# Row sums and second pooled product of each visit in 64x64 tiles, and sums of v by seven full matmuls

## The chip, the cores and the metric

The kernel runs on one core of one Trainium2 chip. The metric is the device time of one launch in microseconds (us), taken as the median over runs. TensorE is called PE in the views, VectorE DVE, ScalarE ACT, GpSimd POOL, and SyncE SP; PEld is TensorE's loading of weights.

## The reference

q, k and v have the shape (8 batches, 8 heads, 576 positions, 64). Two attentions are computed for each head and added, and a two-layer block with SiLU follows.

```python
def _attn_ref(q, k, v):
    factor, Sd, scale = 4, S // 4, 1.0 / np.sqrt(D)
    q_d = q.reshape(B, H, Sd, factor, D).mean(axis=3)     # k_d, v_d alike
    out_d = sm_attn(q_d, k_d, v_d)                        # softmax attention of the 144 pooled rows
    out_up = np.repeat(out_d, factor, axis=2)
    mask = np.abs(pos[:, None] - pos[None, :]) < factor   # a band of 7 positions
    attn = softmax(np.where(mask, scale * q @ k.T, -1e9))
    return out_up + attn @ v

def _moe_ref(x, w_in, w_out):                             # x: 4608 x 512
    h = x @ w_in                                          # 512 -> 2048
    return (h * sigmoid(h)) @ w_out                       # 2048 -> 512
```

## The kernel before, in words

The 64 heads are handled as 32 pairs (two heads of one batch). For a pair p these steps exist, each with its TensorE matmuls, and after them the steps of other engines:

- `T{p}` (`pe_T`): 36 transposes of q and k (L810), evicted by ACT (L565) and then pooled by DVE (L845) into `qd` and `kd`. POOL issues the loads of later pairs' q and k (L676) into buffers that a T frees.
- `S{p}` (`pe_S`): 28 score matmuls (20 of the band, 8 of the pooled rows); ACT takes the exponentials into `Pt` (band) and `Pd` (pooled) (L893), and DVE multiplies `Pt` by the band's mask (L899, called k below).
- `Z{p}` (`pe_Z`): 12 matmuls with the 0/1 columns of `hot` as weights give the row sums of `Pt` and `Pd`; DVE transposes them out of PSUM (`zt`, L964), takes reciprocals (`zr`, L968) and spreads them (`Rb`, L974).
- `PV{p}` (`pe_PV1` and `pe_PV2`): 20 matmuls of `Pt` with v, then 4 and 4 of `Pd` with the pooled v. DVE scales the product by `Rb` (L990), POOL adds the two attentions into `xT` (L1018).
- `VP{p}` (`pe_VP`, only for the first eight pairs): 9 matmuls with the 0/1 matrix `vsel` as weights sum v over groups of four rows; ACT or DVE evicts them into `vd`. For later pairs POOL makes these sums itself (L785, L790).

A matmul has a tile on the 128x128 array: 64x64 (64 rows of the operands, 64 outputs; four such tiles work side by side), 128x64 (two side by side) or 128x128. S, T, PV1 and the first four `Pd` products are 64x64, Z and the last four `Pd` products (`pe_PV2`) are 128x64, the two layers are 128x128, and VP has five matmuls in 128x128 and four in 128x64.

From pair 8 on, the steps of three pairs are put together in a visit `V{n}` on PE, in the order S of pair n, T of pair n+1, PV1 of pair n-2, Z of pair n-1, PV2 of pair n-2. The row sums go to columns 360 to 455 of the second of the two PSUM banks that also hold the PV product. Between visits PE works on the two layers: G1 (groups of 4 matmuls 128x512 with `w_in_sb`, then tanh on ACT, L1043, and the gate on DVE, L1047) and G2 (groups of 4 with `w_out_bf` and `gT`, evicted by ACT, L1100). There are 576 and 592 such matmuls; the last 32 of G2 are of 256 columns.

All orders come from a planner (`Plan.run`) that runs through a list of jobs with costs and due times written into the kernel, and that emits each engine's instructions in the order so found. Nothing of it is decided on the chip. The planner also puts some matmuls of zeros and ones (`dz`) into idle places of the beginning. A job's cost and its marks (when, within a visit, its parts count as finished) only steer this order. Every matmul goes through `mm` (L571).

Of the kernel before, what the change touches and what calls it, by code (L numbers as in the profile page):

```python
# [9 lines left out]
F32 = mybir.dt.float32  # L10
BF16 = mybir.dt.bfloat16
# [15 lines left out]
VP_PE = 8  # L27

SPLIT = 8
CAST2 = 4  # L30
SW = tuple(range(1, NPAIR))
MB = 8
# [16 lines left out]
def D(p, left):  # L49
    return (22 + 1.5 * (p - 3) if p < 4 else 42 + 3 * (p - 7) if p < 8 else 45 + 8 * (p - 7)) - left  # L50
# [444 lines left out]
def bass_hourglass_attn__then__act_silu_kernel(  # L495
# [9 lines left out]
    with kctx:  # L505
        E = kctx.enter_context
        L = Plan()
        P = Prog()
# [31 lines left out]
        kd = sb("kd", [128, 192], BF16, N_T)  # L540
        Pt = sb("Pt", [128, 2, 288], BF16, N_P)
        Pd = sb("Pd", [128, 2, 216], BF16, N_P)
        zt = sb("zt", [128, 96], F32, N_ZR)
        zr = sb("zr", [128, 24], F32, N_ZR)
        Rb = sb("Rb", [128, 768], F32, N_RB)
        xo = sb("xo", [128, 2, 360], F32, N_XO)
# [12 lines left out]
        hot = sb("hot", [128, 3, 68], BF16)  # L559
# [7 lines left out]
        def half(j):  # L567
            return slice(64 * j, 64 * j + 64)

        def mm(out_, lhsT, rhs, r, w, start, stop):  # L570
            P.op("PE", lambda t: t.matmul(out_, lhsT, rhs, start=start, stop=stop, skip_group_check=True), r, w)  # L571

        S = L.slot

# [38 lines left out]
        def constants():  # L613
# [41 lines left out]
            for i, c in enumerate((CO, CO, CO2)):  # L655
                ts(f"vsel{i}", vsel[:, i, :], cpv[:, i % 2, :], 1.5, ALU.is_le, col(c), ALU.mult, rc(c) + rp,
                   [R(f"vsel{i}")], 0.33, ["cpa", "co", "co2"], 7.6)
            fill("pads", [(t[:, a:b], 0.0, [], [R(f"{n}{i}")]) for i in range(N_T)
                          for t, n, a, b in ((kT[i], "kTa", 0, 3), (kT[i], "kTb", 579, 592), (kd[i], "kdp", 144, 192))], -75)
            fill("hot", [(hot[:, i, :], 0.0, [], [R(f"hot{i}")]) for i in range(3)]  # L660
# [135 lines left out]
        def bank(key):  # L796
            return L.bind["bank", key]
# [123 lines left out]

        def after_VP(p):
            def emit(jb):
# [37 lines left out]
        def after_Z(p, key, i, col_):  # L961
            def emitt(jb):
                z, b = S("zr", p), bank(key)[i]
                P.op("DVE", lambda e: e.transpose(zt[z][:, :], PS[:, b, col_:col_ + 96]), [rB[b]], [R(f"zt{z}")])  # L964

            def emit(jb):
                z = S("zr", p)
                P.op("DVE", lambda e: e.reciprocal(  # L968
                    zr[z][:, :].rearrange("p (c b) -> p c b", b=3),
                    zt[z][:, :].rearrange("p (b c) -> p c b", b=3)[:, 0:8, :]), [R(f"zt{z}")], [R(f"zr{z}")])  # L970
# [6 lines left out]
            J(f"zt{p}", "DVE", 0.23, emitt, pre=[f"Z{p}"], bank=[(key, ())], take=[("zr", p)], due=D(p, 4.0))  # L977
# [151 lines left out]
        def split(p):  # L1129
            J(f"T{p}", "PE", 0.42, lambda jb: pe_T(p), mm=36, kind="A", due=D(p, 8.5), **tk(p))  # L1130
            after_T(p)
            if p >= SPLIT:
                return
            J(f"S{p}", "PE", 0.46, lambda jb: pe_S(p), mm=28 + 4 * (p < MB), kind="A", due=D(p, 6.5), **sk(p))
            after_S(p)
            kz = ("z", p)
            J(f"Z{p}", "PE", 0.40, lambda jb: pe_Z(p, bank(kz)[0], 0, True), mm=14, kind="A", due=D(p, 4.5), bank=[(kz, Z_BANKS(p))], **zk(p))
            after_Z(p, kz, 0, 0)
            if p < VP_PE:
                J(f"VP{p}", "PE", 0.68, lambda jb: pe_VP(p), mm=9, kind="A", due=D(p, 4.0), use=[("vb", p)], pre=[f"cv{p}", "vsel0", "vsel1", "vsel2"],  # L1140
                  bank=[(("v", p), V_BANKS(p))])
                after_VP(p)

            def emit(jb):
                bb = bank(("o", p))
                pe_PV1(p, bb)
                pe_PV2(p, bb)
            J(f"PV{p}", "PE", 0.57, emit, mm=28, kind="A", due=D(p, 2.4), bank=[(("o", p), O_BANKS(p))], **merge(vk(p), dict(pre=[f"r{p}"])))
            after_PV(p)

        def visit(n):
            s, t = n < NPAIR, n + 1 < NPAIR
            z = n - 1 if SPLIT <= n - 1 < NPAIR else None
            pv = n - LAG if SPLIT <= n - LAG < NPAIR else None
            marks, at_, kw = {}, 0.0, []
            nm = 28 * s + 36 * t + 28 * (pv is not None) + 14 * (z is not None)
            if s:
                at_ += 0.38
                marks[f"S{n}"] = at_
                kw.append(sk(n))  # L1160
            if t:
                at_ += 0.3
                marks[f"T{n + 1}"] = at_
                kw.append(tk(n + 1))
            if pv is not None:
                at_ += 0.25
                kw.append(vk(pv))
            if z is not None:
                at_ += 0.38
                marks[f"Z{z}"] = at_  # L1170
                kw.append(zk(z))
            if pv is not None:
                at_ += 0.13
                marks[f"PV{pv}"] = at_
            zkey = ("o", pv) if pv is not None else ("zz", n)
            kw.append(dict(bank=[(zkey, (CD,))]))

            def emit(jb):
                if s:
                    pe_S(n)  # L1180
                if t:
                    pe_T(n + 1)
                if pv is not None:
                    pe_PV1(pv, bank(("o", pv)))
                if z is not None:
                    pe_Z(z, bank(zkey)[1], 360, pv is None)
                if pv is not None:
                    pe_PV2(pv, bank(("o", pv)))
            J(f"V{n}", "PE", at_, emit, mm=nm, kind="V", due=n, marks={a: min(1.0, b / at_) for a, b in marks.items()}, thr=8 * (n - THR0),
              **merge(dict(pre=[f"V{n - 1}"] if n > SPLIT else []), *kw))  # L1190
            if s:
                after_S(n)
            if t:
                after_T(n + 1)
            if pv is not None:
                after_PV(pv)
            if z is not None:
                after_Z(z, zkey, 1, 360)


        constants()
# [95 lines left out]
```

## Time and profile before

| what | value |
|---|---|
| median of 3 runs | 341.94 us (341.03 to 342.71) |
| the profiled execution, its own time | 342.31 us |
| its span in the profile | 340.5 us, granted clock 0.97 in the mean |
| matmuls on PE | 4623, each with a weight load |
| stretch up to 11.4 us | loads, constants, first transposes |
| 11.4 to 36.3 us | pairs 0 to 3, no G1 yet |
| 36.3 to 74.9 us | pairs 4 to 7 between groups of G1 |
| 74.9 to 279 us | the visits V8 to V33 between groups of G1 and G2 |
| 279 us to the end | G1 and G2 alone |

Times in the views are in us from the start of the span. A line of the timeline gives the start, the time from first start to last end, the engine, the line of code, the operation, what it writes and reads, its tile, its shape and how many instructions were merged. The ends of matmuls overlap with the next starts, so the cost of a group is read from start to start. In square brackets stands the idle time before and what ended it.

### The profile page before, as it was taken

Reading aid. Unit: us, or ns where it says so; the run is one execution under the profiler, and the core shown is the slowest. Engines: PE = TensorE matmul, PEld = TensorE weight load, DVE = VectorE, ACT = ScalarE, POOL = GpSimd, SP = SyncE. Lnnn points to the kernel's source line nnn. Section 1 sums busy time; section 2 is a strip of 40 time slices with the busy share of each in tenths; the row PEclk is TensorE's granted clock in tenths of the full one; section 3 lists DMA queues with packets and bytes.
Section 4 is the critical chain, followed back from the end, with each engine's and each line's share of the span. In section 5 each row is a group of like instructions: output and inputs, shape, how many; then the busy total and the mean of one; then the engine's idle time right before and its main releaser. Section 6 shows DMA issues by size and latency. Waiting matters only on the chain.

```text
span 340.5 us, 10780 instructions
## 1 busy us (share of the span) xinstructions
PE 326.8 (96%) x4623; PEld 213.9 (63%) x4623; DVE 229.6 (67%) x410; ACT 179.0 (53%) x317; POOL 156.6 (46%) x211
## 2 busy tenths in 40 slices
PE   5587999999999999999999999999999999999996
PEld 2465677865555775587557755785577558866544
DVE  6586989866667885788577857796767556754200
ACT  5542756665544765476447645664656416644221
POOL 7363498435679667970698068704400140000000
PEclk9755999999999999999999999999999999999999
DMA  8997879999878976996398339500100010000112
GB/s 168 175 252 156 255 181 212 198 229 234 172 178 195 213 177 151 209 202 174 76 240 180 81 57 249 115 1 33 66 31 2 33 64 31 2 1 31 62 64 92
DMA packets 70666, 44.59 MB, mean 131 GB/s; under 512 B 45914, under 2 KB 63770, under 8 KB 70618
## 3 DMA queue, kind: packets, MB, share of 16 engines
q1 hardware_dynamic: 56378, 28.00, 30.8%
q0 software_dynamic: 13088, 15.36, 26.2%
q8 instruction: 36, 0.59, 0.7%
q10 hardware_dynamic: 1152, 0.54, 0.7%
q14 instruction: 12, 0.10, 0.1%
HBM read 45.61 MB, written 9.44 MB: 162 GB/s over the span
## 4 chain that ended last, share of the span: by engine, by line
PE 92%; DMA 2%; DVE 2%; issue 2%; POOL 1%; ACT 0%; POOLq 0%
PE PS L571 89%; PE PS L810 3%; DMA qkb<-in_k_dram 2%; DVE Pt L899 1%; POOL qkb L676 0%; DVE qd L845 0%; POOL gT L601 0%; DVE Rb L974 0%; DVE qT L565 0%; DVE kd L845 0%; DVE zt L964 0%; DVE zr L968 0%; ACT osb L1076 0%; DVE vd L565 0%; POOL idw L610 0%
## 5 line engine op out<-in xcount | busy, mean ns | idle before, releaser
L571 PE MATMUL PS<-xT,w_in_sb 128*128 128x512 f32 x576 | 141.2, 399 | 0.0
L571 PE MATMUL PS<-w_out_bf,gT 128*128 128x512 bf16 (+1 forms) x592 | 131.3, 374 | 0.0
L571 PEld LDWEIGHTS PS<-xT,w_in_sb 128*128 128x128 f32 x576 | 106.7, 188 | 24.7 <-DVE gT L1047 0.7
L1047 DVE SCALAR_TENSOR_TENSOR gT<-th,PS 128x512 bf16<-128x512 f32 x144 | 96.9, 683 | 37.0 <-ACT th L1043 36.3
L1043 ACT ACTIVATE th<-PS 128x512 f32<-128x512 f32 x144 | 86.1, 599 | 54.2 <-PE PS L571 46.0
L571 PEld LDWEIGHTS PS<-w_out_bf,gT 128*128 128x128 bf16 x592 | 54.7, 98 | 62.9 <-issue 3.5
L1018 POOL TENSOR_TENSOR xT<-xo 128x576 fp32r<-128x576 f32 (+5 forms) x48 | 43.5, 919 | 51.5 <-DVE xo L990 51.4
L565 POOL CAST vb<-vs 128x640 bf16<-128x640 f32 x32 | 24.4, 767 | 57.3 <-PE PS L571 42.5
L1100 ACT ACTIVATE osb<-PS 128x512 f32<-128x512 f32 x35 | 21.1, 603 | 53.6 <-PE PS L571 53.6
L893 ACT ACTIVATE Pt<-PS 128x576 bf16<-128x576 f32 x32 | 20.8, 649 | 33.0 <-PE PS L571 32.8
L785 POOL TENSOR_TENSOR vt<-vq 128x512 f32<-128x512 f32 x24 | 30.8, 1285 | 10.0 <-DMA vq<-in_v_dram 9.9
L990 DVE TENSOR_TENSOR xo<-PS,Rb 128x720 f32<-128x720 f32 x32 | 28.6, 893 | 5.1 <-PE PS L571 4.9
L974 DVE STREAM_TRANSPOSE Rb<-zr 128x768 f32<-128x768 f32 x32 | 30.9, 964 | 0.1
L899 DVE TENSOR_TENSOR Pt<-Pt,mask 128x576 bf16<-128x576 bf16 x24 | 16.3, 677 | 20.9 <-ACT Pt L893 20.9
L565 ACT ACTIVATE qT<-PS 128x576 bf16<-128x576 bf16 x30 | 19.8, 659 | 9.4 <-PE PS L810 9.4
L810 PE MATMUL PS<-idn,qkb 64*64 64x64 bf16 x1152 | 17.5, 201 | 7.5 <-issue 3.9
L845 DVE TENSOR_REDUCE qd<-qT 128x144 bf16<-128x576 bf16 x32 | 22.9, 716 | 1.5 <-ACT qT L565 1.4
L845 DVE TENSOR_REDUCE kd<-kT 128x144 bf16<-128x576 bf16 x32 | 23.0, 718 | 0.0
L964 DVE STREAM_TRANSPOSE zt<-PS 128x96 f32<-128x96 f32 x32 | 8.8, 274 | 20.2 <-PE PS L571 20.2
L565 ACT ACTIVATE kT<-PS 128x576 bf16<-128x576 bf16 x30 | 20.0, 665 | 1.6 <-PE PS L810 1.6
L810 PEld LDWEIGHTS PS<-idn,qkb 64*64 64x64 bf16 x1152 | 14.2, 115 | 9.5 <-issue 4.5
L676 POOL DMA_DIRECT2D qkb<-in_k_dram x31 | 17.1, 553 | 5.1 <-PE PS L810 5.1
(56 smaller groups left out, 229.3 us busy)
## 6 DMA issues: line engine op xcount, KB each, us to landing
vs<-in_v_dram SPq DMA_DIRECT2D x123, 80.0 KB, 4.6
out_dram<-osb SPq DMA_DIRECT2D x35, 256.0 KB, 3.6
vq<-in_v_dram SPq DMA_DIRECT2D x24, 256.0 KB, 4.3
qkb<-in_q_dram POOLq DMA_DIRECT2D x31, 144.0 KB, 5.0
qkb<-in_k_dram POOLq DMA_DIRECT2D x30, 144.0 KB, 5.4
w_in_sb<-in_moe_w_in_dram POOLq DMA_DIRECT2D x4, 1024.0 KB, 7.4
w_out_bf<-in_moe_w_out_dram POOLq DMA_DIRECT2D x4, 512.0 KB, 14.3
vq<-in_v_dram SPq DMA_DIRECT2D x48, 32.0 KB, 3.9
```

The costliest lines, as they stand in the source:

```text
L565: return e.activation(out_, in_, AF.Copy) if eng == "ACT" else e.tensor_copy(out_, in_)
L571: P.op("PE", lambda t: t.matmul(out_, lhsT, rhs, start=start, stop=stop, skip_group_check=True), r, w)
L785: P.op("POOL", lambda g: g.tensor_tensor(vt[:, :, :], vq[n][:, :, 0:128], vq[n][:, :, 128:256], ALU.add), [R(f"vqm{n}"), R(f"vqe{n}0"), R( ...
L810: P.op("PE", lambda e, o=o, w=w, j=j: e.transpose(o, w, idn[half(j), :]), [R("idn"), R(f"qkb{n}{x}")], [rB[t]])
L845: P.op("DVE", lambda e: e.tensor_reduce(dst, src.rearrange("p (g r) -> p g r", r=4), AX.X, ALU.add), [R(f"{'qk'[x]}T{s}")], [R(f"{'qk'[x]} ...
L893: P.op("ACT", lambda e: e.activation(d[:, :, :], PS[:, b[0]:b[1] + 1, a:e_], AF.Exp, scale=sc), [rB[b[0]], rB[b[1]]], [R(f"P{m}" if local ...
L974: P.op("DVE", lambda e: e.transpose(Rb[n][:, :].rearrange("p (c q) -> p c q", q=32), zr[z][:, :].unsqueeze(2).to_broadcast([128, 24, 32])) ...
L990: P.op("DVE", lambda e: e.tensor_tensor(xo[x][:, :, :], PS[:, bb[0]:bb[1] + 1, 0:360], Rb[u][:, :].rearrange("p (x c) -> p x c", x=2)[:, : ...
L1018: P.op("POOL", lambda g, dst=dst, in0=in0, in1=in1: g.tensor_tensor(dst, in0, in1, ALU.add), [R(f"xo{x}")], xblk(kc, t + a, t + e_))
L1043: P.op("ACT", lambda e: e.activation(th[x][:, :], PS[:, b, :], AF.Tanh, scale=0.5), [rB[b]], [R(f"th{x}")])
L1047: P.op("DVE", lambda e: e.scalar_tensor_tensor(gT[j % 2][:, f, :], th[x][:, :], 1.0, PS[:, b, :], ALU.add, ALU.mult), [rB[b], R(f"th{x}")] ...
L1100: P.op("ACT", lambda e, s=S("osb", n), b=bank(key)[0]: e.activation(osb[s][:, :], PS[:, b, :], AF.Copy, scale=0.5), [rB[bank(key)[0]]], [R ...
```

## The change

In the visits V9 to V31 the row sums and the second pooled product are done in 64x64 tiles. A matmul over 128 rows becomes two over 64 rows. Half j of the rows writes to bank j ("straight"); where the result for the other bank is needed as well, four matmuls with the banks exchanged ("cross") are put behind T, and the first of them waits on a semaphore until the last straight one has ended (`fence`). Of Z, the band's sums and the sums over the last 16 pooled rows now lie in both banks, four row columns in each, so DVE transposes 2 x 96 columns (`zt` is 192 wide); the reciprocal writes the same 24 numbers as before. The order of a visit becomes S, PV1, PV2 straight, Z straight, T, PV2 cross, Z cross; in V31, which has no T, S takes T's place. A visit has 120 matmuls in place of 104 where all parts are there (V10 to V30), V9 has 88 in place of 76, and V31 84 in place of 68. V32 and the first eight pairs keep `pe_Z` and `pe_PV2` as they were.

`pe_VP` replaces its four 128x64 matmuls by two of 128x128, with weights `vend` that ACT copies from `vsel` once, behind its first eviction of q and behind the second pair's evictions. The planner's costs of visits are lowered with it. In the order that comes out, PE has V11 and V18 one group of G2 or G1 later; DVE, in many visits from V11 on, takes L990 ahead of `zt`, and k and the pooling of q ahead of the reciprocal or the `Rb` step, where the order was the other way, and some of these change places with gates of G1 next to them; ACT has some evictions of `kT` behind one of `osb`; POOL and SP have some loads and casts one place earlier or later.

```diff
-        zt = sb("zt", [128, 96], F32, N_ZR)
+        zt = sb("zt", [128, 192], F32, N_ZR)
+        vend = sb("vend", [128, 2, 128], BF16)
...
         def mm(out_, lhsT, rhs, r, w, start, stop):
-            P.op("PE", lambda t: t.matmul(...), r, w)
+            P.op("PE", lambda t: t.matmul(...), r, w, after=fence[:])
+            fence[0] = None
...
             for i in (3, 4):                                    # pe_VP
-                x, sh = (1, 43) if i == 3 else (2, 58)
-                for y in range(2):
-                    one(PS[half(y), b, 128:256], vsel[:, x, 186 - sh:250 - sh], x, i, i == 3, i == 4)
+                mm(PS[:, b, 128:256], vend[:, i - 3, :], vb[n][:, i:i + 6:5, :], [R("vend"), R(f"vb{n}")], [rB[b]], i == 3, i == 4)
...
+        def pe_PV2h(p, bb, cross):
+            m, d = S("P", p), S("vd", p)
+            for h in range(2):
+                for j in range(2):
+                    x = 1 - j if cross else j
+                    mm(PS[half(h), bb[x], 288:360], vd[d][half(j), 2 * h, :], Pd[m][half(j), h, 72 * x:72 * x + 72],
+                       [R(f"vd{d}"), R(f"Pd{m}")], [rB[bb[x]]], False, cross)
+
+        def pe_Zh(p, bb, col_, fresh, cross):
+            m = S("P", p)
+            if cross:
+                seq = [(1, 4, Pd[m], (72, 0), "hot1", f"Pd{m}")]
+            else:
+                seq = [(0, 3 - s, Pt[m], (96 * s, 96 * s), "hot0", f"P{m}") for s in range(3)]
+                seq += [(1, 4, Pd[m], (0, 72), "hot1", f"Pd{m}"), (2, 0, Pd[m], (144, 144), "hot2", f"Pd{m}")]
+            for n, (i, w, src, a, rw_, rp_) in enumerate(seq):
+                c = 72 if cross or i == 2 else 96
+                for h in range(2):
+                    for j in range(2):
+                        x, u = (1 - j if cross else j), w + (4 * j if i != 1 else 0)
+                        mm(PS[half(h), bb[x], col_:col_ + c], hot[half(j), i, u:u + 64], src[half(j), h, a[j]:a[j] + c],
+                           [R(rw_), R(rp_)], [rB[bb[x]]], fresh and n == 0, cross)
...
+                bb = bank(zkey)                                 # visit, new = s and z is not None
+                if pv is not None:
+                    pe_PV1(pv, bb)
+                    pe_PV2h(pv, bb, False)
+                pe_Zh(z, bb, 360, pv is None, False)
+                own = P.streams["PE"][-1]
+                if t:
+                    pe_T(n + 1)
+                else:
+                    pe_S(n)
+                fence[0] = own
+                if pv is not None:
+                    pe_PV2h(pv, bb, True)
+                pe_Zh(z, bb, 360, False, True)
```

More of the change, by code (lines that the diff above doesn't have):

```diff
@@ L29 @@
 SPLIT = 8
+VE, VDUE = 'ACT', 12
 CAST2 = 4
@@ L558, in bass_hourglass_attn__then__act_silu_kernel @@
         nidn = sb("nidn", [128, 64], BF16)
-        hot = sb("hot", [128, 3, 68], BF16)
+        hot = sb("hot", [128, 3, 72], BF16)
         idw = sb("idw", [128, 128], BF16)
         vsel = sb("vsel", [128, 3, 207], BF16)
+        vend = sb("vend", [128, 2, 128], BF16)
         cv = sb("cv", [128, 16], F32)
@@ L570, in mm @@
         def mm(out_, lhsT, rhs, r, w, start, stop):
-            P.op("PE", lambda t: t.matmul(out_, lhsT, rhs, start=start, stop=stop, skip_group_check=True), r, w)
+            P.op("PE", lambda t: t.matmul(out_, lhsT, rhs, start=start, stop=stop, skip_group_check=True), r, w,
+                 after=fence[:])
+            fence[0] = None
+        fence = [None]
         S = L.slot
@@ L657, in constants @@
                    [R(f"vsel{i}")], 0.33, ["cpa", "co", "co2"], 7.6)
+            for i, a in enumerate((143, 128)):
+                const(f"vend{i}", VE, {"ACT": 0.3, "POOL": 0.3}[VE], lambda e, i=i, a=a: copy(
+                    VE, e, vend[:, i, :].rearrange("p (y c) -> p y c", y=2), vsel[:, i + 1, a:a + 64].unsqueeze(1).to_broadcast([128, 2, 64])),
+                      r=[R(f"vsel{i + 1}")], w=[R("vend")], pre=[f"vsel{i + 1}"], due=VDUE)
             fill("pads", [(t[:, a:b], 0.0, [], [R(f"{n}{i}")]) for i in range(N_T)
@@ L976, in emitb @@
                     zr[z][:, :].unsqueeze(2).to_broadcast([128, 24, 32])), [R(f"zr{z}")], [R(f"Rb{n}")])
-            J(f"zt{p}", "DVE", 0.23, emitt, pre=[f"Z{p}"], bank=[(key, ())], take=[("zr", p)], due=D(p, 4.0))
+            J(f"zt{p}", "DVE", 0.34 if two else 0.23, emitt, pre=[f"Z{p}"], bank=[(key, ())], take=[("zr", p)], due=D(p, 4.0))
             J(f"r{p}", "DVE", 0.26, emit, pre=[f"zt{p}"], use=[("zr", p)], due=D(p, 3.9))
@@ L1139, in split @@
             if p < VP_PE:
[L1140 removed]
+                J(f"VP{p}", "PE", 0.68, lambda jb: pe_VP(p), mm=7, kind="A", due=D(p, 4.0), use=[("vb", p)], pre=[f"cv{p}", "vsel0", "vsel1", "vsel2", "vend0", "vend1"],
                   bank=[(("v", p), V_BANKS(p))])
@@ L1155, in visit @@
             marks, at_, kw = {}, 0.0, []
-            nm = 28 * s + 36 * t + 28 * (pv is not None) + 14 * (z is not None)
+            new = s and z is not None
+            if new:
+                nm = 28 * s + 36 * t + 32 * (pv is not None) + 24
+            else:
+                nm = 28 * s + 36 * t + 28 * (pv is not None) + 14 * (z is not None)
             if s:
-                at_ += 0.38
+                at_ += 0.37
                 marks[f"S{n}"] = at_
                 kw.append(sk(n))
+            if new:
+                at_ += 0.19 + 0.225 * (pv is not None)
             if t:
@@ L1165, in visit @@
             if pv is not None:
-                at_ += 0.25
+                at_ += 0.03 if new else 0.25
                 kw.append(vk(pv))
             if z is not None:
-                at_ += 0.38
+                at_ += 0.03 if new else 0.38
                 marks[f"Z{z}"] = at_
                 kw.append(zk(z))
+            if new:
+                at_ += 0.1
+                marks[f"Z{z}"] = at_
             if pv is not None:
-                at_ += 0.13
+                at_ += 0.0 if new else 0.13
                 marks[f"PV{pv}"] = at_
@@ L1178, in emit @@
             def emit(jb):
-                if s:
+                if s and (t or not new):
                     pe_S(n)
+                if not new:
+                    if t:
+                        pe_T(n + 1)
+                    if pv is not None:
+                        pe_PV1(pv, bank(("o", pv)))
+                    if z is not None:
+                        pe_Z(z, bank(zkey)[1], 360, pv is None)
+                    if pv is not None:
+                        pe_PV2(pv, bank(("o", pv)))
+                    return
+                bb = bank(zkey)
+                if pv is not None:
+                    pe_PV1(pv, bb)
+                    pe_PV2h(pv, bb, False)
+                pe_Zh(z, bb, 360, pv is None, False)
+                own = P.streams["PE"][-1]
                 if t:
                     pe_T(n + 1)
+                else:
+                    pe_S(n)
+                fence[0] = own
                 if pv is not None:
[L1184 to L1188, printed above, removed]
+                    pe_PV2h(pv, bb, True)
+                pe_Zh(z, bb, 360, False, True)
             J(f"V{n}", "PE", at_, emit, mm=nm, kind="V", due=n, marks={a: min(1.0, b / at_) for a, b in marks.items()}, thr=8 * (n - THR0),
@@ L1197, in visit @@
             if z is not None:
-                after_Z(z, zkey, 1, 360)
+                after_Z(z, zkey, 2 if new else 1, 360)
         constants()
```

20 lines of the change are left out of this document (15 added, 5 removed).

## The prediction

> **What bounds the kernel now.** I read the page first: shares of engines, slices, chain of waits.
>
> ```profile
> PE 326.8 (96%) x4623; PEld 213.9 (63%) x4623; DVE 229.6 (67%) x410; ACT 179.0 (53%) x317; POOL 156.6 (46%) x211
> PEclk9755999999999999999999999999999999999999
> PE 92%; DMA 2%; DVE 2%; issue 2%; POOL 1%; ACT 0%; POOLq 0%
> ```
>
> PE is busy for 96% of the span and carries 92% of the chain, at full granted clock from the fifth slice on. So what PE saves in a visit is saved at the end, unless a new wait takes it. Next comes the timeline of PE over one visit, with the layer matmuls behind it.
>
> ```profile
> 168.38 0.35 PE L571 MATMUL PS<-qT,kT 64*64 64x58 bf16 x20
> 168.56 0.27 PE L571 MATMUL PS<-qd,kd 64*64 64x144 bf16 x8
> 168.66 0.48 PE L810 MATMUL PS<-idn,qkb 64*64 64x64 bf16 x36
> 168.95 0.35 PE L571 MATMUL PS<-Pt,vb 64*64 64x58 bf16 x20
> 169.12 0.22 PE L571 MATMUL PS<-Pd,vd 64*64 64x72 bf16 x4
> 169.27 0.32 PE L571 MATMUL PS<-Pt,hot 128*64 128x96 bf16 x6
> 169.42 0.28 PE L571 MATMUL PS<-Pd,hot 128*64 128x96 bf16 x6
> 169.54 0.23 PE L571 MATMUL PS<-Pd,vd 128*64 128x72 bf16 x4
> 169.71 4.49 PE L571 MATMUL PS<-w_out_bf,gT 128*128 128x512 bf16 x20
> 174.13 0.35 PE L571 MATMUL PS<-qT,kT 64*64 64x58 bf16 x20
> ```
>
> Read from start to start, the visit takes 169.71 - 168.38 = 1.33 us and recurs every 5.75. In 64x64 tiles 36 transposes take 0.29, 8.1 ns each or 0.032 per four. The four `Pd` products at 169.12 should take the same 0.03, but 0.15 pass before the first row sum: 0.12 is the change to 128x64. The second six row sums take 0.12 (0.04 a pair), the first six 0.15. The last four products take 0.17, where pairs at 72/96 of 0.04 need 0.06: 0.11 is the change to 128x128.
>
> **Part 1, Z and PV2 in the visits.** Removed: from the end of the first `Pd` products (169.15) to 169.71, 0.56 us. Added: 32 matmuls of 64x64 in groups of four: four groups of 96 columns, one of 72 (Z straight), one of 72 (PV2 straight), two of 72 behind T. No row shows 96 columns in 64x64. The group of 64 columns takes 0.032; the eight `qd,kd` matmuls take 0.10 for a group of 144 and one of 72, which leaves 0.066 for 144. Between these 96 columns take 0.044; the bounds are 0.032 and 0.066. Sum: 4 x 0.044 + 4 x 0.033 + 0.11 for the one change of tile left = 0.42. Saved 0.14 per visit (0.05 to 0.19), the same in V9 and V31. 23 visits give **-3.2 us** (-1.2 to -4.3).
>
> **Part 2, the fence.** The first cross matmul waits for the last straight one; queued behind it are the other cross matmuls and the next layer group, and `zt` and L990 on DVE wait for these. A 64x64 matmul of 72 columns lasts 203 ns in the groups, and ACT's exponential at 168.88 starts some 0.05 after the S before it ends, so the release comes about 0.25 after the last straight start. T lies between: 36 transposes, 0.29 (in V31 S, 0.28). So it costs **0**, with 0.04 to spare. If the release took 0.1 longer, 23 x 0.06 = 1.4 us; with no cover at all 0.25 x 23 = 5.8.
>
> **Part 3, what moves.** T ends some 0.43 later in the visit (about 169.59 in this one, not 169.14). ACT evicts it from 169.84, as it is busy with the exponentials until then: no loss. POOL's loads of q and k wait for T, and are buffered pairs ahead. PV1 and Z come earlier, but read what DVE and POOL finished in the visit before. `zt` doubles: 0.274 us for 96 columns; bounded by 0 and by twice, I take +0.1, as `Rb` needs 964 ns for 768. DVE's `kd` ended at 173.04 and S used it at 174.31, so 1.27 us cover that. The cover is thinner in G1 right after a run of visits, where DVE works without a break, 0.67 a gate beside a group of 0.91:
>
> ```profile
> 189.57 2.68 DVE L1047 SCALAR_TENSOR_TENSOR gT<-th,PS 128x512 bf16<-128x512 f32 x4
> ```
>
> PE already waits on such gates ten times, 2.7 us of weight loads in the list of waits, mostly hidden. PE comes 0.14 earlier and DVE 0.1 later per visit: 0 to 0.3 for each of four runs; I take **+0.3** in all (0 to 1.2).
>
> **Part 4, VP.** The first four VPs lie where PE waits anyway ("issue" of 1.1 to 2.1 us at 16.6, 21.9, 28.4): 0. The other four:
>
> ```profile
> 39.14 0.69 PE L571 MATMUL PS<-vb,vsel 128*128 128x128 bf16 x9
> 39.76 0.32 PE L571 MATMUL PS<-mbias,nidn 64*64 64x288 bf16 x4
> 47.08 0.69 PE L571 MATMUL PS<-vb,vsel 128*128 128x128 bf16 x9
> 47.70 1.21 PE L571 MATMUL PS<-xT,w_in_sb 128*128 128x512 f32 x4
> ```
>
> Nine take 0.62. Seven of 128 columns, at a quarter of the 0.22 of a 512-column one, take 0.39, and then a change of tile (0.11) at 39.76, or up to that much for the first f32 weights at 47.70: 0.12 saved each. At 38.27 Z follows in the same 128x64, so nothing is saved there. **-0.4 us** (-0.1 to -0.7). The two `vend` copies fall into ACT's idle 1.39 and 1.07 us of the first pairs: 0.
>
> **Part 5, a stall that may go.** In V10 PE waits for `kd`, because k took 2.54 us (0.40 to 0.46 in most visits) while POOL ran casts and sums:
>
> ```profile
> 81.37 2.54 DVE L899 TENSOR_TENSOR Pt<-Pt,mask 128x576 bf16<-128x576 bf16 x1
> 86.48 0.29 PE L571 MATMUL PS<-qd,kd 64*64 64x144 bf16 x8 [0.59 <-DVE kd L845]
> ```
>
> S's first part took 0.94 here, 0.18 elsewhere: 0.76 lost. POOL's cast at 81.63 follows loads that wait for T, which now ends 0.2 later, so k may get through first. Half of it: **-0.4 us**; ends -0.76 and +0.8 (k runs into POOL in another visit).
>
> **Part 6, code.** PE gets 22 x 16 + 12 - 16 = 348 more matmuls and as many weight loads. Its code comes in pieces:
>
> ```profile
> q8 instruction: 36, 0.59, 0.7%
> ```
>
> 9246 PE instructions against 36 transfers are 257 each, so 696 more are nearly three more. At 209.96 a visit stood for half a microsecond on "issue" in mid-visit; in these runs 248 instructions pass per 5.75 us, and 280 will per 5.61. I take **+0.3** (-0.5, that stall gone, to +2.5, one more in each run).
>
> **Sum.** -3.2 + 0 + 0.3 - 0.4 - 0.4 + 0.3 = -3.4. Against the profiled execution's 342.31 (span 340.5 and 1.8 around it) that is 338.9. That execution is 0.37 above the median of 341.94, so I predict 338.5.
>
> **A rule against it.** The Trainium skill, "TensorEngine Tiling (Array Packing)", section "Instruction Overhead", says that every matmul costs about 60 cycles, so that one with a single column takes as long as one with 60. At the 2.4 GHz of its page "TensorE: Matmul & The Clock Gate" that is an estimated 25 ns, and 32 matmuls would take 0.8 us in place of 0.31. This trace does not agree: its 36 transposes take 8.1 ns each.
>
> **Rivals.** (a) *Each matmul has its own price.* If the 32 matmuls took the 20 ns that a row sum takes now (six in 0.12), the part would be 0.64 + 0.11 = 0.75 against 0.56: 23 x 0.19 = 4.4 us more, less 0.8 from parts 4 and 5: 345.5. It decides from 14 ns each ((0.56 - 0.11)/32). For it: no row has 64x64 row sums, and the two halves of the rows read one tile. Against: 8.1 and 9 ns in T and S. The rule above is this case; 5%. (b) *Code becomes the bound in runs of visits.* A piece of 256 now lasts 5.9 us there and will last 5.13. The three stalls of the start ended 5.4 and 6.5 us apart, so a piece can take that long when loads are dense. At 5.4, 24 pieces lose 0.27 each, 6.5 us: 344.7. It decides from 5.3. Against: with 5.9 us between them only one of some 24 pieces was late; 7%. (c) *The gain is eaten, no change.* The fence costs 0.06, DVE 0.3 per run, code one stall per run: 338.5 + 1.4 + 0.9 + 1.2 = 342.0; 17%. (d) *The planner's new order alone*, V11 and V18 a group later, costs or gives nothing by itself, as PE has other work ready; it is within the range.
>
> **How the numbers follow.** My forecast has 71%: -5.1 (all good ends of parts 4 to 6 with 3.2) gives 336.8; the fence, half of DVE's bound and one more code stall give 341.2. With part of (c) the range 336.8 to 341.3 holds 8 in 10. A measurement can tell about 0.5%, 1.7 us, from no change: faster is below 340.2, slower above 343.6. Faster 0.71, same 0.17, slower 0.12 (a and b).
>
> **What would show it.** Right: visits of 1.19 us from S to the next layer group, a period of 5.61, no 128x64 rows from 92 us to 270, groups of four row sums 0.04 apart, a cross matmul within 0.01 of T's end, `zt` at 0.37, VPs of 0.5. Wrong: an idle time before the cross matmuls, "issue" in several visits, new waits of PE on `kd` or on gates, or row sums 15 ns or more apart.

## The result and the profile after

The changed kernel takes 339.04 us in the median of 21 executions (337.98 to 342.57), beside 341.24 us for the kernel before (21 executions): a ratio of 0.9945 (95% interval 0.9925 to 0.9964), so 2.2 us faster. The forecast of 338.5 lies 0.54 below, and its range holds the median. Its saving of 3.4 us was too large all the same: the median of the three runs that the forecast set out from lay 0.7 above this median of 21. A second series of the changed kernel (below) gave 340.12 beside 341.37, 1.25 us.

The profiled execution took 338.79 us, with a span of 337.0. From its page, in the order of the prediction's lines (shares of engines, PE's clock by slices, chain of waits, transfers of PE's code):

```profile
PE 325.8 (97%) x4971; PEld 212.5 (63%) x4971; DVE 234.5 (70%) x410; ACT 179.9 (53%) x319; POOL 154.5 (46%) x211
...
PEclk9755999999999999999999999999999999999999
...
q8 instruction: 39, 0.64, 0.8%
...
PE 95%; DMA 2%; issue 2%; POOL 1%; ACT 0%; POOLq 0%
```

PE still carries the chain, with 348 more matmuls and three more pieces of code. DVE's share rose from 67% to 70%, 4.9 us of work, though only `zt` was meant to grow, by 23 x 0.1 = 2.3 us. The timeline of PE over one visit that nothing held up (V29):

```profile
240.14 0.35 PE L573 MATMUL PS<-qT,kT 64*64 64x58 bf16 x20
240.32 0.27 PE L573 MATMUL PS<-qd,kd 64*64 64x144 bf16 x8
240.42 0.32 PE L573 MATMUL PS<-Pt,vb 64*64 64x58 bf16 x20
240.58 0.24 PE L573 MATMUL PS<-Pd,vd 64*64 64x72 bf16 x8
240.64 0.32 PE L573 MATMUL PS<-Pt,hot 64*64 64x96 bf16 x12
240.78 0.26 PE L573 MATMUL PS<-Pd,hot 64*64 64x96 bf16 x8
240.85 0.48 PE L820 MATMUL PS<-idn,qkb 64*64 64x64 bf16 x36
241.15 0.22 PE L573 MATMUL PS<-Pd,vd 64*64 64x72 bf16 x4
241.18 0.22 PE L573 MATMUL PS<-Pd,hot 64*64 64x72 bf16 x4
241.34 1.04 PE L573 MATMUL PS<-w_out_bf,gT 128*128 128x512 bf16 x4
```

From start to start this visit takes 1.20 us (1.192 unrounded), as forecast. The twelve row sums of `Pt` take 0.13, 0.043 per four; the cross matmul starts 0.30 after T does, which is T's own length. But few visits look so. V19, the first of its run, in the same timeline:

```profile
160.22 0.35 PE L573 MATMUL PS<-qT,kT 64*64 64x58 bf16 x20
...
160.96 0.60 PE L820 MATMUL PS<-idn,qkb 64*64 64x64 bf16 x36
161.37 0.23 PE L573 MATMUL PS<-Pd,vd 64*64 64x72 bf16 x4
...
161.56 3.63 PE L573 MATMUL PS<-w_out_bf,gT 128*128 128x512 bf16 x16
```

T begins 0.74 after S here (0.71 in V29) and lasts 0.41 instead of 0.30: 1.34 us in all. The trace of instructions shows why: T's weight loads have waits of their own, for the loads of q and k and for its freed banks, and waits that do not fit into the weight load are instructions of PE's stream, which show where the stream has no lead: in V19 one of 0.05 us stands between T's first two weight loads, which start 0.125 us apart. Of the visits V10 to V30 only V19, V23, V27 and V30, the first ones of later runs, have such a one in T, and they take 1.33 to 1.40 us.

To see where the time went, PE's starts are summed by kind from V8's first matmul to the last matmul. In the profiles of the experiments the first record of a G2 group is missing behind 21 visits and behind six stretches of G1. In before and after, where none is missing, the second matmul of such a group starts 0.226 us behind the first, and that is taken off the visit or the stretch ahead each time and counted as G2. G2 is then 121.97 to 121.99 everywhere but in e4, where it is 123.66. e1 is not in the table: its profiled execution ran slower, at a granted clock of 0.93, and took 345.65 us.

| profile | V8 starts | V8 to last matmul | visits | mean of V10 to V30 | G1 |
|---|---|---|---|---|---|
| before | 74.88 | 262.68 | 33.46 | 1.402 | 107.24 |
| after | 73.69 | 260.39 | 30.19 | 1.258 | 108.21 |
| e2 visits alone | 75.42 | 260.76 | 30.38 | 1.266 | 108.40 |
| e3 fence uncovered | 74.35 | 267.26 | 37.52 | 1.590 | 107.76 |
| e4 T's waits early | 74.36 | 269.97 | 36.82 | 1.574 | 109.49 |
| e5 the same, code shifted | 73.92 | 259.74 | 29.49 | 1.221 | 108.28 |
| e6 after, code shifted | 74.67 | 260.40 | 30.43 | 1.270 | 107.98 |
| e7 old order | 75.19 | 260.84 | 30.25 | 1.261 | 108.61 |
| e8 after, code shifted more | 74.94 | 262.78 | 32.31 | 1.273 | 108.48 |
| e9 k first | 73.86 | 259.26 | 30.15 | 1.256 | 107.13 |
| e10 k first and e5 | 75.60 | 259.43 | 29.99 | 1.249 | 107.47 |
| e11 after again | 74.01 | 260.62 | 30.58 | 1.277 | 108.07 |
| e12 before, k first | 74.46 | 261.99 | 33.07 | 1.384 | 106.94 |

The profiled pair differs by 3.5 us of span: 1.2 before V8, 3.3 in the visits, and 1.0 given back in G1. Two questions follow: what the visits lose against 1.19 us, and why groups of G1 that nobody changed take longer.

### The profile page after: what moved, and what is told of

The parts are those of the page before. It is cut to its first block, busy times and chain, and to the rows that moved or that the text cites. A ratio compares the mean times of both kernels' runs of the same rounds, so it can differ in the third digit from the quotient of the medians.

```text
span 337.0 us, 11476 instructions
## 1 busy us (share of the span) xinstructions
PE 325.8 (97%) x4971; PEld 212.5 (63%) x4971; DVE 234.5 (70%) x410; ACT 179.9 (53%) x319; POOL 154.5 (46%) x211
## 4 chain that ended last, share of the span: by engine, by line
PE 95%; DMA 2%; issue 2%; POOL 1%; ACT 0%; POOLq 0%
PE PS L573 91%; PE PS L820 4%; DMA qkb<-in_k_dram 2%; POOL gT L607 0%; POOL qkb L686 0%; ACT osb L1119 0%; POOL idw L616 0%; POOL cv L607 0%; POOLq L607 0%; POOLq L1350 0%
## 5 line engine op out<-in xcount | busy, mean ns | idle before, releaser
L1061 POOL TENSOR_TENSOR xT<-xo 128x576 fp32r<-128x576 f32 (+5 forms) x48 | 41.7, 883 | 52.1 <-DVE xo L1033 52.1
L567 POOL CAST vb<-vs 128x640 bf16<-128x640 f32 x32 | 23.0, 723 | 55.1 <-PE PS L573 42.0
L909 DVE TENSOR_TENSOR Pt<-Pt,mask 128x576 bf16<-128x576 bf16 x24 | 19.1, 798 | 22.3 <-ACT Pt L903 22.3
L820 PE MATMUL PS<-idn,qkb 64*64 64x64 bf16 x1152 | 18.3, 202 | 6.0 <-issue 4.0
L800 POOL TENSOR_TENSOR vd<-vt 128x256 bf16<-128x256 f32 x24 | 19.0, 794 | 0.5
```

The lines of the kernel that those rows point to most:

```text
L567: return e.activation(out_, in_, AF.Copy) if eng == "ACT" else e.tensor_copy(out_, in_)
L820: P.op("PE", lambda e, o=o, w=w, j=j: e.transpose(o, w, idn[half(j), :]), [R("idn"), R(f"qkb{n}{x}")], [rB[t]])
L1061: P.op("POOL", lambda g, dst=dst, in0=in0, in1=in1: g.tensor_tensor(dst, in0, in1, ALU.add), [R(f"xo{x}")], xblk(kc, t + a, t + e_))
```

## The experiments

**Each half alone.** e1 keeps the old visits, e2 the old `pe_VP`.

```diff
-            new = s and z is not None
+            new = False                                 # e1_vp_only
```
```diff
-                mm(PS[:, b, 128:256], vend[:, i - 3, :], ...)
+                x, sh = (1, 43) if i == 3 else (2, 58)  # e2_visits_only
+                for y in range(2):
+                    one(PS[half(y), b, 128:256], vsel[:, x, 186 - sh:250 - sh], ...)
```

> Only the sums of v by seven matmuls and the two copies of weights; the visits are as before. In the profiled pair V8 starts at 73.7 us where it was 74.9. Theory (the seven matmuls shorten the stretch where PE has work all the time, 36 to 57 us): two VPs of 0.38 in place of 0.62 and two saved 0.1 or less, V8 0.5 to 0.7 us earlier relative to the first layer group, the time 0.4 to 0.7 us below before (ratio 0.998 to 0.999). Rival (the start decides: when pieces of code and loads arrive): V8's start scatters by 1 us or more from execution to execution, and the time is the same as before or moves by more than 1 us either way.

> Only the visits are changed; VP keeps its nine matmuls. Theory (gains add up): from V8 to the end 2.3 us shorter than before as in the changed kernel's profile (265.6 to 263.3), the time 1.5 to 2.3 us below before, ratio 0.993 to 0.996. Rival (most of the measured gain came from the start): less than 0.8 us, ratio above 0.9975.

e1 took 340.87 us, ratio 0.9976 (0.9951 to 1.0001); e2 took 340.27, ratio 0.9966 (0.994 to 0.9992), beside 341.36 before. The halves, 0.5 and 1.1 us, add up to about what the whole saves; e1's interval holds 1, so its half is not shown by the times alone. e2 fell short of the 1.5 to 2.3 us expected: the visits bring one third of their -3.2 in the median. e2's profile has the same losses as after's: visits of 1.266 in the mean and G1 at 108.40. VP has nothing to do with them.

**The fence without its cover.** T goes back behind S, so that nothing lies between the last straight and the first cross matmul.

```diff
                 pe_S(n)
+                pe_T(n + 1)                             # e3_fence_bare
                 ...
                 pe_Zh(z, bb, 360, pv is None, False)
-                pe_T(n + 1)
                 fence[0] = own
```

> As the changed kernel, but T goes back to its place behind S, so nothing lies between the last straight row sum and the cross matmuls that wait for it. Theory (release 0.25 us after the last straight start, hidden by T's 0.29): an idle time of about 0.25 us before the cross matmuls in 22 visits (V31 keeps its cover), less 0.02 to 0.1 because T's own waits are then passed while PE still works on the layer matmuls; visits of 1.40 us, 4 to 5 us above the changed kernel, 1 to 2 us above before. Rival (the release is quick, the cover is not needed): idle below 0.1, the time as in the changed kernel or below it.

345.7 us, ratio 1.0117 (1.0078 to 1.0156). PE's timeline in V21:

```profile
177.48 0.36 PE L573 MATMUL PS<-Pt,hot 64*64 64x96 bf16 x12
177.66 0.26 PE L573 MATMUL PS<-Pd,hot 64*64 64x96 bf16 x8
178.00 0.23 PE L573 MATMUL PS<-Pd,vd 64*64 64x72 bf16 x4
```

Eight row sums that take 0.07 in V29 are followed by the cross matmul after 0.34: the release costs 0.27 when nothing covers it. The shortest visits are 1.49 us, 0.3 above 1.19 and 0.09 above the 1.40 expected. The time lies 5.6 to 6.7 us above the changed kernel (345.7 against 340.12 and 339.04), where 4 to 5 were expected; the prediction's price for "no cover at all" was 5.8, and its 0 for the covered fence holds.

**T's waits taken early.** The first matmul of S also waits for T's loads and banks, so that PE's stream meets them where it is still ahead of its matmuls.

```diff
+                early = [the loads of q and k that T reads, the last readers of its two banks]
+                fence[:] = early                        # ahead of pe_S(n): e4_t_hoist
```

> As the changed kernel, but the first matmul of S also waits for what T will wait for (loads of q and k, the freed banks), so that T carries no wait. Theory A (T now stands so late in the visit that PE's instruction stream has no lead left, and its semaphore waits, which the start of a visit used to hide, show: 0.02 us in most visits, 0.14 in the first of each run): all visits 1.19 to 1.21, sum of V10 to V30 down by 0.7 to 1.3 us, the time 0.7 to 1.3 below the changed kernel, ratio to before 0.991 to 0.993. Theory B (the longer visits, 1.21 to 1.41 instead of 1.19, come from code that arrives late): they stay as they are, the same time as the changed kernel.

V19 fell from 1.34 to 1.21 us, so the waits were most of the loss there. Yet the kernel took 345.74 us, ratio 1.0134 (1.0089 to 1.018). Its profiled execution, which with 349.05 us was 3.3 us longer still, shows stalls of another kind, a small one at 104.06 us (0.76) and three large ones in PE's timeline between 204 and 223 us:

```profile
204.42 4.26 PE L573 MATMUL PS<-w_out_bf,gT 128*128 128x512 bf16 x19 [1.51 <-issue]
...
212.43 0.23 PE L820 MATMUL PS<-idn,qkb 64*64 64x64 bf16 x5 [2.68 <-issue]
...
222.66 0.38 PE L820 MATMUL PS<-idn,qkb 64*64 64x64 bf16 x22 [1.82 <-issue]
```

"issue" in the middle of T is a wait for nothing the profile shows. If PE's instructions are counted in the trace (two per matmul, one per separate wait), these places lie at the end of a piece of 256. Around the first two, ends were 3.8 and 4.4 us apart, while loads of v, q and k ran; the transfer of the next piece began 5.8 us after the end at 204.20 and 7.3 us after the one at 212.44. Where few loads run, it begins 0.7 to 0.9 us after.

**The same with the ends of the pieces moved.** Matmuls of ones ahead of the first group of G2 (at 71.9 us), overwritten by that group, push all later instructions of PE on: twelve in e5 (on e4) and in e6 (on the changed kernel), 64 in e8.

```diff
+                    if (j, tt, part) == (0, 0, 0):
+                        for i in range(12):             # 64 in e8
+                            mm(PS[half(i % 2), b, 0:8], dz[:, 0:64], dz[:, 0:8], [R("dz")], [rB[b]], True, True)
```

> The kernel with the waits of T's loads and banks moved to the first matmul of S (345.7 us), with twelve more matmuls of ones (128x64, 8 columns; overwritten by the layer group that follows) ahead of the first w_out group at 71.9 us. They cost 0.2 to 0.5 us and push every later instruction of PE 24 places on, so that the places where a piece of 256 PE instructions ends fall elsewhere: two of them 2.9 us apart at 197 us, before the loads start again, and none closer than 5.2 us from 200 to 222 (before: 3.8 and 4.4 us apart at 200 and 204). Theory code (the late pieces alone made that kernel slow): the issue stalls of 1.5, 2.7 and 1.8 us between 204 and 223 go, and the time falls to 337.5 to 339.5 us. Rival hoist (the early waits hold PE back, or the runs were otherwise disturbed): 345 to 346 us, whatever the places.

> The changed kernel with the same twelve matmuls. Its two piece ends 2.9 us apart at 202 us, where loads are dense, move to 110.5, 196 and 243 us, where there are few. Theory code (the 4 of 21 executions near 342.3 us are those in which a piece after 202 us comes late): no execution near 342, the others 0.2 to 0.5 above 338.8, median 339.0 to 339.4. Rival (these executions have another cause, such as the chip's state): again about one in five near 342.

> The changed kernel with 64 such matmuls, 1.3 to 2.2 us by themselves at 71.9 us, which push the later instructions 128 places on: piece ends then come 2.9 us apart at 87 us and 3.05 apart at 134 us, both amid dense loads, with 4.6 and 4.1 us after them. Theory code: issue stalls of 1 to 6 us in visits or groups between 87 and 100 us or between 134 and 148 us, and 342 to 347 us in most executions. Rival (code in pieces is not what decides): only the price of the added matmuls, 340.3 to 341.3 us, and no such stall.

e5: the three stalls are gone, and the time fell from 345.74 to 340.03 us (338.29 to 344.3), ratio 0.995 (0.9925 to 0.9976). So late code made e4 slow, and not the early waits. Its visits are the shortest of all, 29.49 us, 0.7 and 1.1 less than in the two profiles of the changed kernel and 0.9 less than in e6, which has the same shift without the early waits. That is what T's waits cost there, as far as they can be moved. The visits still have 1.221 in the mean, not 1.19: in most of them T takes 0.32 us instead of 0.30 though no wait is left in it, and the cause of that stays open. The median expected (337.5 to 339.5) was missed; the stretch ahead of V8 varies by more than that (see below).

e6: 339.44 us, 7 executions, none near 342 and one at 341.34. That tells nothing: e11 repeats the changed kernel itself, and of its 12 executions none lies near 342.3 either. The 4 of 21 in the first series are not tied to these pieces; their cause stays open.

e8: 342.32 us, ratio 1.003 (1.0009 to 1.0051). The matmuls cost 1.3 us by themselves (72.00 to 73.34). No stall came at 87 or at 134 us, where the ends lie 2.9 us apart, so the expectation failed in its places. One stood elsewhere, at an end only 5.5 us after the last:

```profile
75.22 0.48 PE L820 MATMUL PS<-idn,qkb 64*64 64x64 bf16 x36
77.67 4.27 PE L573 MATMUL PS<-w_out_bf,gT 128*128 128x512 bf16 x19 [1.97 <-issue]
```

The transfer of that piece began 2.8 us after the end before it. So the distance of two ends does not decide by itself; it is the distance together with what the transfer meets. At 87 and 134 us the transfers had begun 1.1 and 1.9 us ahead of the end, out of a stretch of layer matmuls with few instructions.

**The planner's order.** The new visits and VP with the old prices in the planner, so that PE, DVE, POOL and SP keep the sequence of the kernel before.

```diff
-            J(f"zt{p}", "DVE", 0.34 if two else 0.23, ...)
+            J(f"zt{p}", "DVE", 0.23, ...)               # e7_old_order; marks and price of V{n} as before, too
```

> The changed kernel's instructions in the order of the kernel before: the planner is given the old prices of the visits and of zt, and so PE, DVE, POOL and SP have the same sequence as before the change (V11 and V18 a layer group earlier than in the changed kernel). Theory order (the planner's new order made the first-layer groups after runs of visits dearer): their sum from V8 on falls from 108.2 to 107.2 - 107.5 us, and the time to about 338. Rival load (DVE is later because zt is longer and PE comes earlier, whatever the order): it stays at 108.0 or above and the time at 339.

G1 stayed at 108.61, the time at 339.83 us (0.9951; 0.9926 to 0.9975): theory order falls. What e7 shares with the changed kernel is found below: in the last visit of a run, at 147, 182 and 217 us, k takes 1.40 to 1.47 us.

**k ahead of zt.** DVE has 4.9 us more work in after, and the groups of DVE show that 2.9 of it is k (`Pt<-Pt,mask`), which the change did not touch: in the visits from V9 on it takes 0.81 us in the mean instead of 0.69. The last visit of the run, V22, in the timelines of DVE and then of POOL, in before:

```profile
182.48 0.91 DVE L990 TENSOR_TENSOR xo<-PS,Rb 128x720 f32<-128x720 f32 x1
183.31 0.27 DVE L964 STREAM_TRANSPOSE zt<-PS 128x96 f32<-128x96 f32 x1
183.50 0.42 DVE L899 TENSOR_TENSOR Pt<-Pt,mask 128x576 bf16<-128x576 bf16 x1
```
```profile
183.56 1.45 POOL L1018 TENSOR_TENSOR xT<-xo 128x576 fp32r<-128x576 f32 x1
```

and the same two timelines in after:

```profile
179.74 0.91 DVE L1033 TENSOR_TENSOR xo<-PS,Rb 128x720 f32<-128x720 f32 x1
180.56 0.37 DVE L998 STREAM_TRANSPOSE zt<-PS 128x192 f32<-128x192 f32 x1
180.86 1.41 DVE L909 TENSOR_TENSOR Pt<-Pt,mask 128x576 bf16<-128x576 bf16 x1
```
```profile
180.72 1.23 POOL L1061 TENSOR_TENSOR xT<-xo 128x576 fp32r<-128x576 f32 x1 [0.15 <-DVE xo L1033]
```

In before k starts 0.06 ahead of POOL's sum, takes 0.42, and the sum 1.45. In after `zt` pushes k back by 0.1, and POOL is free earlier (its cast of v starts 0.82 us after S instead of 1.15, as PV1 releases v earlier); the sum starts 0.14 ahead of k, takes 1.23, and k takes 1.41. The same happens at 147 and 215 us. The gates of G1 stand behind k. e9 swaps the two neighbours on DVE, at nine places, and nothing else:

```diff
+        seq = list(L.run(pick))
+        dve = [jb for jb in seq if jb.ran == "DVE"]
+        for a, b in zip(dve, dve[1:]):                  # a = zt{p}, b = k{p+1}, from V10 on
+            if a.name.startswith("zt") and b.name[0] == "k" and ...:
+                i, j = seq.index(a), seq.index(b)
+                seq[i:j + 1] = seq[i + 1:j + 1] + [a]
-        for jb in L.run(pick):
+        for jb in seq:
```

> The changed kernel with two neighbours on DVE swapped where zt stands just ahead of k (from V10 on): k (the product with the mask) first, then zt. Nothing else changes its order. In the changed kernel k takes 1.40 us in the last visit of each run (at 147, 181 and 215 us), where the kernel before takes 0.42: there POOL's sum into xT starts 0.07 after xo ends and k starts 0.14 later, behind zt. Theory start order (of k and POOL's sum the one that starts later waits for the other, and the lost microsecond goes into the first-layer groups that follow): with k directly behind xo it starts first and takes 0.4 to 0.5 us, POOL's sum some 0.2 longer, the first-layer groups sum to 107.2 - 107.6 us instead of 108.2, and the time falls by 0.6 to 1.2 us to 338.0 - 338.4. Rival load (zt's longer time and PE's earlier arrival make DVE late, whatever the order): k gets shorter but zt and the gates behind it come no earlier, the groups stay at 108 and the time at 339.

338.16 us (6 executions, 337.32 to 340.4), ratio 0.9918 (0.9889 to 0.9947). The timelines of DVE and POOL at the same place of e9:

```profile
179.22 0.91 DVE L1033 TENSOR_TENSOR xo<-PS,Rb 128x720 f32<-128x720 f32 x1
180.04 0.45 DVE L909 TENSOR_TENSOR Pt<-Pt,mask 128x576 bf16<-128x576 bf16 x1
180.41 0.38 DVE L998 STREAM_TRANSPOSE zt<-PS 128x192 f32<-128x192 f32 x1
```
```profile
180.21 1.38 POOL L1061 TENSOR_TENSOR xT<-xo 128x576 fp32r<-128x576 f32 x1
```

k takes 0.45, POOL's sum 0.15 longer, and G1 falls to 107.13, 1.1 and 0.9 less than in the two profiles of the changed kernel. It falls where k was swapped. PE's timeline of the run behind V22, in before and in after:

```profile
182.37 13.00 PE L571 MATMUL PS<-xT,w_in_sb 128*128 128x512 f32 x56
195.21 1.90 PE L571 MATMUL PS<-w_out_bf,gT 128*128 128x512 bf16 x8
```
```profile
179.55 13.21 PE L573 MATMUL PS<-xT,w_in_sb 128*128 128x512 f32 x56
192.60 1.69 PE L573 MATMUL PS<-w_out_bf,gT 128*128 128x512 bf16 x7
```

From start to start the same 56 matmuls take 12.85 us in before, 13.05 in after and 12.81 in e9. The runs behind V14, V18 and V26 take 15.01, 13.26 and 13.03 in after and 14.74, 12.85 and 12.85 in e9. The run behind V30, where nothing was swapped, keeps its 14.72 to 14.75.

Of k and the sum, the one that starts first goes through. This is what the Trainium skill says in "SBUF — State Buffer", section "SBUF: two separate sides": of a DVE operation with two SBUF inputs and a GpSimd operation that reads SBUF, the one that starts first holds their common port pair for the whole instruction. The trace agrees, with 0.45 against 1.41 us. But the starts in a profile do not tell it to the last hundredth. Where the sum starts only 0.04 to 0.05 us ahead, it is k that goes through, as in V21 of before (timelines of DVE and of POOL):

```profile
176.85 0.40 DVE L899 TENSOR_TENSOR Pt<-Pt,mask 128x576 bf16<-128x576 bf16 x1
```
```profile
176.81 1.51 POOL L1018 TENSOR_TENSOR xT<-xo 128x576 fp32r<-128x576 f32 x1
```

With 0.07 ahead, in e7 at 147 us, the sum goes through, and k takes 1.47. And in V10 of before k starts 0.26 us ahead of POOL's cast and takes 2.54 all the same; POOL was issuing a load when k started, and which of its steps held k up is not shown.

What PE waited for with its weight loads, from 100 to 270 us, in the lists of waits of before, after and e9 (total, times, longest):

```profile
PEld PS L571 <- DVE gT L1047: 2.0, 8, 0.3
```
```profile
PEld PS L573 <- DVE gT L1090: 3.5, 14, 0.4
```
```profile
PEld PS L573 <- DVE gT L1090: 1.3, 5, 0.3
```

The waits on gates grew from 8 to 14 with the change, and fell to 5 with the swap.

**The swap with e5, the changed kernel again, and the swap in the kernel before.** e10 is the swap on e5; e12 applies the same lines to the kernel before, where they change three places.

> The same swap in the kernel that moves the waits of T's loads and banks to the first matmul of S and has twelve more matmuls ahead of the first w_out group (340.0 us). If both losses are what they seem: visits of 1.19 to 1.22 us, first-layer groups of 107.3, and from V8 to the last matmul 258.9 us (259.7 without the swap, 260.4 in the changed kernel); undisturbed executions at 337.3 to 337.8 us, median 338.0 to 339.2. If the swap does nothing: 338.3 at best and 340.0 in the median, as before.

> The changed kernel itself beside the two. By the runs so far: 338.0 to 340.3 us in four of five executions and 342.1 to 342.6 in the fifth, median 339.0; k of 1.40 us again in the last visit of each run, and first-layer groups of 108.0 to 108.4 us. If the late executions belong to this order of pieces of code, one to four of some twelve are late here again; if they were a chance of that one series, none.

> The kernel before with the same swap: k ahead of zt, which there changes the order at three places only (the last visits of three runs). There k already starts 0.06 us ahead of POOL's sum and takes 0.42 us. Theory start order (the microsecond came with the change): nothing to win, first-layer groups of 106.9 to 107.3 us as before (107.2), time within 0.4 of the kernel before. Rival (the swap is worth a microsecond in any kernel, so that the change lost nothing there): groups of 106.3 us or less and 340.2 to 340.5 us beside 341.3.

e10: 338.61 us (337.0 to 341.06), ratio 0.9926 (0.99 to 0.9952). G1 is 107.47, but the visits with 29.99 did not keep e5's 29.49; V14, V15 and V21 took 1.36 to 1.48 in this profile. Nothing shows that it beats e9. e11: 340.12 us (337.9 to 341.86), ratio 0.9958 (0.9933 to 0.9984), 1.1 above the median expected; k again takes 1.41 us in the last visits, and G1 108.07. e12: 341.57 beside 340.99, ratio 1.0007 (0.998 to 1.0034): no gain. The runs of G1 behind its three swapped visits, V18, V22 and V26, take 13.74, 12.85 and 12.85 us, the same as in before. That G1 sums to 106.94 and not to 107.24 comes from the run behind V14 (14.69 against 14.96), where nothing was swapped and k took 0.40 us instead of 1.34. So what the swap brings in e9 came with the change, but for the 0.2 us behind V14.

## Why the prediction was right or wrong

**Right: the price of the matmuls (part 1).** A visit with nothing in its way went from 1.327 to 1.192, 0.135 against the 0.14 of the sum; 23 visits make 3.1 us. Rival (a) is out: the row sums of `Pt` take 11 ns each, the other products 8 to 9, below its point of 14.

**Right: the fence (part 2).** T covers it; without T it costs 0.3 per visit, where the prediction named 0.25.

**The step that failed: part 3, twice.** The step from "T ends some 0.43 later in the visit" to "no loss" asked who waits for T, and not what T itself waits for. Late in the visit T's waits meet a PE stream that has no lead left. V10 to V30 average 1.258 where 1.192 was meant, a loss of 1.4 us, against 0.3 in before (1.341 without its two stalls, where 1.327 is clean): 1.1 us more. In after's profile some 1.2 of the 1.4 stand at T; taking its waits early won back 0.7 to 1.1 in e5, and why the rest stays is open. And the +0.3 for the gates in G1 is 0.97 in the profiled pair (107.24 to 108.21; 108.0 to 108.6 in the other profiles with T as cover and `zt` ahead of k, e4 apart, whose stalls reach into G1). The named causes, PE earlier and `zt` longer, are still there in e9, where G1 is 107.13, no more than before; by themselves they cost nothing that shows. The cost is the mechanism of part 5, k running into POOL, which the sum had only for V10, though it gave its price ("k runs into POOL in another visit", +0.8).

**Mis-sized: VP (part 4).** Measured 0.6 in the profiled pair instead of 0.4. In after, the two VPs between layer groups take 0.37 and 0.38 instead of 0.62:

```profile
46.43 0.45 PE L573 MATMUL PS<-vb,vsel 128*128 128x128 bf16 x5
46.72 0.28 PE L573 MATMUL PS<-vb,vend 128*128 128x128 bf16 x2
46.80 1.17 PE L573 MATMUL PS<-xT,w_in_sb 128*128 128x512 f32 x4
```

The f32 group starts 0.08 after the first of the two `vend` matmuls, so the 0.11 kept for a change of tile is not there. e1's median has 0.5, within an interval that reaches no change.

**Better than half: V10 (part 5).** Its stall of 0.78 us is gone whole: V10 takes 1.19 us in every profile with the new visits but e3, and 2.11 in the profiles of before and e12. In e3, where T again stands early in the visit, V10 takes 2.03 and k 2.20, which bears out the reason given; that half of it was taken was a guess.

**Code (part 6).** 39 transfers instead of 36, as worked out. In before V25 lost 0.5 us at such an end; in after's profile no stall of that size stands in a visit, but PE stood still for 0.58 us at another end, at 44.10 us in the PV product of an early pair, where before has no stall and e12 has one of 0.45. Rival (b) did not come true for the change, but e4's profiled execution shows its mechanism with 6.0 us at three pieces: the kernel is that near to it. The Trainium skill, "Runtime: NRT & Kernel Launch", section "Instruction fetch mechanics", has the blocks of 256 instructions, and says that fetching them is hidden because issue is slower than the fill. The count agrees; that it is hidden does not hold here, with 1.5, 2.7 and 1.8 us in e4. Rival (c), a gain eaten up, had one of its three parts come true, DVE's.

**The sum as it mostly is.** Matmuls -3.1, VP -0.6, V10 -0.8, longer visits (T's waits above all) +1.1, gates +1.0: -2.4, where two series measured -2.2 and -1.25. The profiled pair shows -3.5, near the forecast, because V25's stall (0.5) and 0.6 of the beginning came on top. That beginning makes most of the spread: the three "issue" stalls at 15, 21 and 28 us sum to 4.4 us in after's profile and to 5.9 in e11's, the same kernel, and V8 starts anywhere from 73.7 to 75.6 in kernels that hardly differ up to there. No difference below half a microsecond between the experiments' times is read for that reason; the table's sums from V8 on are. That the forecast lies within 0.54 us of the median is in part luck: it set out from 341.94, and from 341.24, the median of 21, the same saving would have given 337.8.

## What to carry to other kernels

When a step moves later in an engine's order, price what that step waits for as well as who waits for it: waits that a lead used to hide come to light. When DVE and POOL both work from SBUF, look at which of two neighbours starts first; a tenth of a microsecond in the starts made one of them take a whole one longer, and swapping two neighbours got the lost time back. And before many short instructions are added, look for places where two ends of a code piece fall close together amid dense loads.

## What the runs showed of the hardware that was not expected

- Of k and POOL's sum, the one that starts 0.06 to 0.17 us later loses: k 0.42 to 0.45 or 1.41 us, the sum 1.23 or 1.38 to 1.45. A lead of the sum of 0.04 to 0.05 us is not enough: k then takes 0.39 to 0.40, and the sum up to 1.51.
- PE's code comes in pieces of 256 instructions. The transfer of the next piece begins 0.7 to 0.9 us after an end where few loads run and up to 7.3 us after where they are dense. It takes 0.9 to 1.7 us in e4, where PE went on 1.2 to 1.6 us after it had ended.
- A semaphore between two matmuls of PE costs 0.27 us uncovered. Taking T's waits ahead of S, where PE's stream has a lead, shortened the first visit of a run by 0.12 us (V19: 1.34 to 1.21).
- Matmuls of 64x64 with 96 columns come every 11 ns in four tiles; a change from 128x128 bf16 to 128x128 f32 shows no gap (the f32 group starts 0.08 us after the first of two bf16 matmuls of 128 columns).
